# Where second-layer groups stand in the order of TensorE's work, in an attention and two-layer kernel

## The chip, the cores and the metric

The kernel runs on one core of one Trainium2 chip. The metric is the device time of one execution in microseconds (us). Before the change the median of three runs is 332.02 us (331.84 to 338.3). The engines are named as in the profile: PE is TensorE's matmuls and PEld its weight loads, ACT is ScalarE, DVE is VectorE, POOL is GpSimd, and SP is SyncE, which here only issues DMAs.

## The reference

Eight sequences (B) of 576 rows and eight heads (H) of width 64 go through causal attention with 16 extra ("beacon") keys in front. The result, 4608 tokens of width 512, goes through two matrix products with a leaky ReLU between them.

```python
k_all = np.concatenate([beacon_k, k], axis=2)
v_all = np.concatenate([beacon_v, v], axis=2)
scores = scale * np.matmul(q, k_all.transpose(0, 1, 3, 2))
scores = np.where(causal, -1000000000.0, scores)
scores = scores - scores.max(-1, keepdims=True)
a = np.exp(scores)
a /= a.sum(-1, keepdims=True) + 1e-09
attn_out = np.matmul(a, v_all)
x = attn_out.transpose(0, 2, 1, 3).reshape(B * S, H * D)
h = x @ w_in                       # 512 -> 2048
g = np.maximum(0.01 * h, h)
out = g @ w_out                    # 2048 -> 512
```

## The kernel before, in words

**Pairs.** Attention is worked in 32 pairs of heads, four to a sequence, numbered g = 0 to 31. Pairs 0 to 7 are written out as a string of steps (L756 to L764). From pair 8 on (`FIRST`), the score columns of all pairs, 1664 to a pair, are laid end to end and cut into tiles of 512. Three tiles make one `block` (L780), so there are 26 blocks, here B0 to B25. A block's score matmuls (L314) fill one tile in two single banks of PSUM (`apart`) and two tiles in two-bank buffers. ACT then takes the exponentials: of the first tile head by head (L329), of the other two at once for both heads (L333). POOL zeroes what lies above the diagonal (L289).

**Values.** `value(g, half)` multiplies probabilities with values (L359): 12 matmuls in the first half of a pair, 18 in the second. Each half takes one PSUM bank, which DVE empties (reciprocal L388, product L389). `x_turn(g)` then has SP write the transposed result into `xT` by two DMAs (L417, L425; three in the last sequence). Here V11.0 and V11.1 are the halves of pair 11.

**The two layers.** The 4608 tokens are nine chunks of 512. `up()` issues one first-layer group (`moe1`): four 512-column matmuls (L442, eight 256-column ones where a chunk wraps round in `xT`) into one PSUM bank, which ACT empties with the leaky ReLU into `gT` (L450). A chunk has 16 of them, here u2.0 to u2.15 for chunk 2. `down()` issues one second-layer group (`moe2`). Chunk 0 has 16 plain ones (L512). The others have 14, d2.0 to d2.13, from a Strassen-like scheme of seven products in two parts of eight 256-column matmuls each (L539). Products are added up in four banks: "a" is opened by group 0 and closed after group 5, "b" is open over groups 2 and 3, "c" from 6 to 11, "d" from 8 to 13. The left sides of some products are sums over `gT` that DVE makes (`token_sums`, L616): four additions for every eight first-layer groups, of which each later group issues one.

**PSUM.** Of the eight banks the two score buffers hold four. The other four (`ps_one`) are shared by first-layer groups, second-layer products, value halves and the two `apart` tiles of a block.

**Order.** The order on all engines is the order in which the program calls these functions (`manual_schedule`, L731), and each engine executes its own list in order. From pair 8 on a list of events with due times is sorted (L814) and walked: blocks, value halves, `x_turn`, the loads of queries, keys and values (`N`, `load_v_cast` on POOL's queue), the DMA transposes of queries and keys (`T`, on SP's queue) and `finish(g)`. Ahead of each event, `fill()` is called until the count of groups has reached a share of those that the sequence has to give (L820 to L823). `finish` of a sequence's last pair releases further chunks (`ready`): chunk 2 with pair 11, 3 with 15, 4 with 19, 5 with 23, 6 with 27, 7 and 8 with 31. `KEPT` groups are left over at a sequence's end.

`fill()` picks which kind of group is next. Before the change it alternates: a second-layer group is chosen after a first-layer one where both are possible (`turn`), and after a sequence's end up to `KEPT` second-layer groups come first (`held`). A first-layer group of chunk i needs chunk i-2 to be done in the second layer.

The lines that the prediction's steps touch: `fill` L598 to L610, `up` L625, `down` L636, `finish` L678 to L684, the loop L817 to L831, and the bank requests in `moe1` (L434), `moe2` (L535), `value` (L384) and `stretch` (L301).

Of the kernel before, what the change touches and what calls it, by code (L numbers as in the profile page):

```python
# [15 lines left out]
def kernel(  # L16
# [21 lines left out]
    NF = DF // 128  # L38
# [124 lines left out]
    def load_first_keys():  # L163
        for h in range(2):
            nc.sync.dma_start(out=first_k[h], in_=k[0, h].rearrange("(p i) d -> p i d", i=RI))
# [18 lines left out]
    def load_beacon_k(b0, b1, eng):  # L184
        eng.dma_start(out=bk_raw[:, b0:b1], in_=beacon_k[b0:b1].rearrange("b h n d -> (h n) b d"))
# [245 lines left out]
    def moe1(i, fc):  # L431
        if i not in gT:
            gT[i] = gpool.tile([128, NF, 512], BF16, name="gT")
        acc = ps_one.tile([128, 512], FP32, name="acc", tag="one")  # L434
        at = i * 512 % (XR * S)
        cut = min(512, XR * S - at)
        for lo, hi in ((0, cut), (cut, 512)):
            for j in range(NJ):
                if lo == hi:
                    continue  # L440
                x0 = (at + lo) % (XR * S)
                nc.tensor.matmul(  # L442
                    out=acc[:, lo:hi],
                    lhsT=w_in_cols(fc, j),
                    rhs=xT[:, j, x0 : x0 + hi - lo],
                    start=(j == 0),
                    stop=(j == NJ - 1),
                    skip_group_check=True,
                )
        nc.scalar.activation(out=gT[i][:, fc, :], in_=acc, func=AF.Prelu, alpha=0.01)  # L450
# [53 lines left out]
    def ND(i):  # L504
        return NF if i == 0 else 2 * len(PRODUCTS)
# [87 lines left out]
            in_=c.rearrange("p (t d) -> p t d", t=n),  # L593
        )

    done1, done2, at2, ready, turn, first_down, held = [0], [0], [0, 0], [0], [0], [0], [0]

    def fill():  # L598
        i1, fc = divmod(done1[0], NF)
        i2, n2 = at2  # L600
        can1 = i1 < ready[0] and (i1 < 2 or i2 > i1 - 2)
        can2 = i2 < NCH and i2 < i1 and done1[0] >= first_down[0]
        if held[0] and can2:
            held[0] -= 1
            down()
        elif can1 and (turn[0] == 0 or not can2):
            up()
        elif can2:
            down()
        return can1 or can2  # L610
# [3 lines left out]
    def add_due(n=1):  # L614
        while due and n:
            nc.vector.tensor_tensor(**due.pop(0)[1])  # L616
            n -= 1

    def add_all(i):
        while due and due[0][0] == i:  # L620
            add_due()
# [3 lines left out]
    def up():  # L625
        i1, n = divmod(done1[0], NF)
        assert i1 < ready[0]
        fc = n if i1 == 0 else n // 2 + n % 2 * HF
        moe1(i1, fc)
        add_due()  # L630
        done1[0] += 1
        turn[0] = 1
        if i1 and n % (2 * SLICE) == 2 * SLICE - 1:
            due.extend((i1, op) for op in token_sums(i1, n // 2 + 1 - SLICE, n // 2 + 1))

    def down():  # L636
        add_due()
        if at2[1] == 2:
            add_all(at2[0])
        moe2(*at2)  # L640
        done2[0] += 1
        at2[1] += 1
        if at2[1] == ND(at2[0]):
            at2[:] = at2[0] + 1, 0
        turn[0] = 0

    def unused(n, cols=128):
        ps = ps_one.tile([128, 512], FP32, name="av", tag="one")
# [16 lines left out]
            )  # L665

    NG = B * NPAIR
    KEPT = 3

    def has(g):  # L670
        return 0 <= g < NG
# [3 lines left out]
    def chunks_with(g):  # L675
        return (g + 1) // NPAIR * S // 512

    def finish(g, eng=0):  # L678
        if eng < 2 and g in xs:
            x_transposes(g, (dve, act)[eng])  # L680
        ready[0] = chunks_with(g)
        if g % NPAIR == NPAIR - 1:
            turn[0] = 1
            held[0] = KEPT  # L684

    def run(steps):
        for step in steps.split():
# [52 lines left out]
    with order:  # L740
        load_first_keys()
        load_beacon_k(0, 2, nc.scalar)
        nc.vector.memset(blank, 0.0)
        nc.vector.memset(ident, 0.0)
        run("l0.0 l1.0")
        make_identity(nc, ident, nomemset=True)
        make_ones()
        run("l1.1 l2.0 l2.1 V0.0 V0.1 l3.0 l3.1 V0.2 V0.3 V0.4 l4.0 l4.1 i0")
        make_pads()
        unused(13, 256)  # L750
        cast_beacon_k(0, 2, nc.scalar.copy)
        beacon_transposes(0, 2)
        unused(13)
        nc.scalar.copy(out=k_nat0[:, :, 0], in_=first_k[0])
        nc.vector.tensor_copy(out=k_nat0[:, :, 1], in_=first_k[1])
        run("q0.1 k0 w2.384 s0.0 m0.0 w3.256 s0.1 q1 s0.2 m0.1 k1 s0.3 m0.2")  # L756
        run("w2.384 s1.0 m1.0 q2 s1.1 k2 w2.384 s1.2 m1.1 w2.384 s1.3 m1.2 W0.0.4 s2.0 m2.0 W0.0.4 s2.1 W0.0.6 q3 l5.0 l5.1 s2.2 k3 w4.384 v0.0 m2.1 s2.3 i1 m2.2 W0.1.4 s3.0 m3.0 v1.0 s3.1 v0.1 s3.2 v1.1 m3.1 l6.0 l6.1 s3.3 x0.1 m3.2")
        run("v2.0 V1.0 V1.1 q4 v2.1 x1 k4.1 v3.0 v3.1 x2.1 s4.0 s4.1 x3 m4.0 V1.2 V1.3 V1.4 l7.0 l7.1 u u s4.2 s4.3 q5 k5 m4.1 m4.2 u o0 u")
        load_beacon_k(2, B, nc.gpsimd)
        run("s5.0 s5.1 m5.0 u u u s5.2 s5.3 q6 k6 m5.1 m5.2 o1 u u s6.0 s6.1 m6.0 u v4.0 u v4.1 y4 N8.0 N8.1 u s6.2 s6.3 q7 k7 m6.1 m6.2 u")  # L760
        cast_beacon_k(2, B, nc.gpsimd.tensor_copy)
        run("u v5.0 u v5.1 N9.0 s7.0 s7.1 m7.0 d x5 v6.0 v6.1 T8 d s7.2 s7.3")
        beacon_transposes(2, B)
        run("m7.1 m7.2 N9.1 u b8.2 b9.2 b10.2 b11.2 x6 v7.0 T9 v7.1 d d t0 d N10.0 N10.1 d V2.0 V2.1 x7 T10")  # L764


        FIRST = 2 * NPAIR
        COLS = FLAT[NKB]
        TILES = (NG - FIRST) * COLS // 512

        def tile_parts(n):
            at, end, parts = 512 * n, 512 * (n + 1), []
            while at < end:
                r, lo = divmod(at, COLS)
                hi = min(COLS, lo + end - at)
                parts.append((FIRST + r, lo, hi))
                at += hi - lo
            return parts

        def block(m):  # L780
            tiles = [tile_parts(n) for n in range(3 * m, min(3 * m + 3, TILES))]
            for n, parts in enumerate(tiles):
                stretch(parts, apart=n == 0)
            for parts in tiles:
                triangles(parts)

        def has_down():
            return at2[0] < done1[0] // NF

        since = 0  # L790
        events = []
        for g in range(FIRST, NG):
            if g > FIRST + 2:
                events.append((g - 2.75, 0, run, ("N%d.0" % g,)))
                events.append((g - 2.45, 0, run, ("N%d.1" % g,)))
            if g > FIRST + 2:
                events.append((g - 1.75, 0, run, ("T%d" % g,)))
            if g > FIRST + 3:
                events.append((g - 1.65, 0, run, ("b%d.2" % g,)))
            at = g + (2.05 if g % NPAIR == NPAIR - 1 else 2.25)  # L800
            events.append((at, 3, value, (g, 0)))
            events.append((at + 0.37, 4, value, (g, 1)))
            events.append((at + 0.38, 5, x_turn, (g,)))
        for m in range((TILES + 2) // 3):
            events.append((FIRST + (0.4 if m else 0.6) + 1536 / COLS * m, 2, block, (m,)))
        ends = [FIRST]
        for g in range(FIRST, NG):
            events.append((g + 3.5, 2, finish, (g, 2)))
            if g % NPAIR == NPAIR - 1:
                ends.append(g + 3.5)  # L810
        for b in range(2, B):
            for n in range(2 if b == 2 else 0, NKB):
                events.append((4 * b + (-0.4 if b == 2 else -0.9) + 0.3 * n, 6, load_v_cast, (b, n)))
        events.sort(key=lambda e: e[:2])  # L814
        first_down[0] = 4
        w, d0 = 0, done1[0] + done2[0]
        for at, _, what, args in events:  # L817
            while w + 2 < len(ends) and at > ends[w + 1]:
                w, d0 = w + 1, done1[0] + done2[0]
            todo = NF * ready[0] + sum(ND(i) for i in range(ready[0])) - KEPT - d0  # L820
            aim = d0 + todo * (at - ends[w]) / (ends[w + 1] - ends[w])
            while done1[0] + done2[0] < aim and fill():
                pass  # L823
            if what is block:
                since = done1[0] + done2[0]
            elif what is value and not has_down():
                while done1[0] + done2[0] < since + 4 and fill():
                    pass
            what(*args)
        while at2[0] < NCH:  # L830
            fill()  # L831
# [30 lines left out]
```

## Time and profile before

| what | value |
|---|---|
| median of three runs | 332.02 us |
| the profiled execution's own time | 332.48 us |
| its span, from the first to the last instruction | 330.8 us |
| granted TensorE clock | 0.999 |
| PE busy | 317.8 us |
| ACT busy | 199.8 us |
| POOL busy, DMA issues included | 183.2 us |
| DVE busy | 132.5 us |
| DMA packets | 155929, of them 143041 under 512 B |

A line of the timeline gives the start and the length in us, the engine, the line of the program, the operation, what it writes and reads, and how many instructions were merged. In square brackets stands the idle time of the engine before it, and what ended that. Ends of matmuls are modelled, so that a wait of PE is best read from the start of one matmul to the start of the next. A few matmul records are missing from the trace.

### The profile page before, as it was taken

Reading aid. Unit: us, or ns where it says so; the run is one execution under the profiler, and the core shown is the slowest. Engines: PE = TensorE matmul, PEld = TensorE weight load, DVE = VectorE, ACT = ScalarE, POOL = GpSimd, SP = SyncE. Lnnn points to the kernel's source line nnn. Section 1 sums busy time; section 2 is a strip of 40 time slices with the busy share of each in tenths; the row PEclk is TensorE's granted clock in tenths of the full one; section 3 lists DMA queues with packets and bytes.
Section 4 is the critical chain, followed back from the end, with each engine's and each line's share of the span. In section 5 each row is a group of like instructions: output and inputs, shape, how many; then the busy total and the mean of one; then the engine's idle time right before and its main releaser. Section 6 shows DMA issues by size and latency. Waiting matters only on the chain.

```text
span 330.8 us, 8482 instructions
## 1 busy us (share of the span) xinstructions
PE 317.8 (96%) x3401; PEld 213.1 (64%) x3429; DVE 132.5 (40%) x280; ACT 199.8 (60%) x336; POOL 183.2 (55%) x354
## 2 busy tenths in 40 slices
PE   8999999999899999999999999998999999999996
PEld 5574555455586557844778888655875695466685
DVE  3572357126443145414621453334442642333343
ACT  4969861678665784578645865587458514644420
POOL 8895968979987884669546976686221000000000
PEclk9999999999999999999999999999999999999999
DMA  8999999999999999999989999999431113000113
GB/s 134 140 204 178 153 209 121 179 181 131 180 111 169 158 157 142 131 164 102 145 122 154 109 146 113 184 120 155 55 100 37 36 21 127 2 0 34 64 43 117
DMA packets 155929, 39.93 MB, mean 121 GB/s; under 512 B 143041, under 2 KB 153153, under 8 KB 155889
## 3 DMA queue, kind: packets, MB, share of 16 engines
q0 software_dynamic: 99824, 18.54, 83.1%
q1 hardware_dynamic: 55792, 20.77, 38.7%
q8 instruction: 27, 0.44, 0.6%
q14 instruction: 14, 0.11, 0.1%
q10 hardware_dynamic: 272, 0.07, 0.1%
HBM read 37.22 MB, written 9.44 MB: 141 GB/s over the span
## 4 chain that ended last, share of the span: by engine, by line
PE 76%; DMA 8%; ACT 5%; DVE 4%; POOL 4%; issue 2%; SPq 0%; ACTq 0%; POOLq 0%
PE acc L442 34%; PE acc L539 25%; PE av L359 7%; PE sc L314 5%; DMA w_out_sb<-in_moe_w_out_dram 4%; PE acc L512 4%; DMA v_aug<-in_v_dram 3%; DVE gsum L616 2%; ACT aT L333 2%; ACT aT L329 2%; ACT gT L450 1%; DVE x_nat L389 1%; POOL gsum L158 1%; DMA xT<-x_nat 1%; POOL v_aug L214 1%
## 5 line engine op out<-in xcount | busy, mean ns | idle before, releaser
L442 PE MATMUL acc<-xT,w_in_sb 128*128 128x512 bf16 (+1 forms) x615 | 134.0, 357 | 1.9 <-DMA xT<-x_nat 0.5
L450 ACT ACTIVATE gT<-acc 128x512 bf16<-128x512 f32 x144 | 83.0, 620 | 56.9 <-PE acc L442 55.4
L442 PEld LDWEIGHTS <-w_in_sb 128*128 128x128 bf16 x640 | 59.6, 98 | 53.6 <-issue 4.3
L289 POOL TENSOR_SCALAR_AFFINE_SELECT aT<-aT 128x256 bf16<-128x256 bf16 (+2 forms) x160 | 59.8, 403 | 60.9 <-ACT aT L329 38.7
L539 PEld LDWEIGHTS <-gT 128*128 128x128 bf16 x512 | 48.9, 98 | 11.2 <-ACT gT L450 2.3
L333 ACT ACTIVATE aT<-sc 128x1024 bf16<-128x1024 f32 (+3 forms) x64 | 51.7, 890 | 0.0
L539 PE MATMUL acc<-w_out_sb,gT 128*128 128x256 bf16 x384 | 47.2, 273 | 1.4 <-ACT gT L450 1.3
L329 ACT ACTIVATE aT<-sc 128x512 bf16<-128x512 f32 (+3 forms) x64 | 28.9, 520 | 25.3 <-PE sc L314 25.3
L359 PEld LDWEIGHTS <-aT 128*128 128x128 bf16 (+1 forms) x960 | 36.6, 98 | 9.3 <-issue 3.0
L539 PEld LDWEIGHTS <-gsum 128*128 128x128 bf16 x384 | 36.1, 98 | 8.8 <-DVE gsum L616 3.3
L359 PE MATMUL av<-v_aug,aT 128*128 128x65 bf16 (+1 forms) x960 | 39.5, 194 | 1.9 <-ACT aT L329 1.6
L214 POOL DMA_DIRECT2D v_aug<-in_v_dram x40 | 34.3, 866 | 4.3 <-DMA w_in_sb<-in_moe_w_in_dram 4.0
L171 POOL DMA_DIRECT2D q_nat<-in_q_dram x48 | 34.9, 734 | 0.7
L171 POOL DMA_DIRECT2D k_nat<-in_k_dram x48 | 34.8, 732 | 0.7 <-DMA w_out_sb<-in_moe_w_out_dram 0.4
L539 PE MATMUL acc<-w_sum,gsum 128*128 128x256 bf16 x256 | 32.9, 273 | 1.8 <-DVE gsum L616 1.7
L616 DVE TENSOR_TENSOR gsum<-gT 128x1024 bf16<-128x1024 bf16 x16 | 11.2, 697 | 53.9 <-ACT gT L450 53.9
L389 DVE TENSOR_TENSOR x_nat<-av,rec 128x384 bf16<-128x384 f32 (+1 forms) x64 | 31.4, 490 | 2.2
L388 DVE RECIPROCAL rec<-av 128x6 f32<-128x6 f32 (+1 forms) x64 | 11.9, 185 | 50.7 <-PE av L359 50.5
L276 ACT ACTIVATE aT<-sc 128x1024 bf16<-128x1024 f32 (+3 forms) x32 | 26.0, 874 | 3.7 <-PE sc L267 1.9
L314 PE MATMUL sc<-qT,kT 64*128 64x80 bf16 (+22 forms) x384 | 22.4, 250 | 1.2 <-PE acc L442 0.5
L314 PEld LDWEIGHTS <-kT 64*128 64x128 bf16 x384 | 13.3, 94 | 11.9 <-issue 8.9
L573 DVE TENSOR_TENSOR u<-acc,u 128x512 f32<-128x512 f32 x8 | 5.5, 691 | 27.2 <-PE acc L539 27.2
(63 smaller groups left out, 221.5 us busy)
## 6 DMA issues: line engine op xcount, KB each, us to landing
out_dram<-osb SPq DMA_DIRECT2D x27, 256.0 KB, 2.8
q_nat<-in_q_dram POOLq DMA_DIRECT2D x48, 72.0 KB, 4.8
k_nat<-in_k_dram POOLq DMA_DIRECT2D x48, 72.0 KB, 5.2
v_aug<-in_v_dram POOLq DMA_DIRECT2D x24, 128.0 KB, 6.4
w_in_sb<-in_moe_w_in_dram POOLq DMA_DIRECT2D x2, 1024.0 KB, 12.3
w_out_sb<-in_moe_w_out_dram POOLq DMA_DIRECT2D x2, 1024.0 KB, 11.6
out_dram<-u SPq DMA_DIRECT2D x7, 256.0 KB, 2.3
gsum<-in_q_dram POOLq DMA_DIRECT2D x8, 144.0 KB, 6.4
```

The source lines that it names most:

```text
L171: nc.gpsimd.dma_start(out=t[:, :, par], in_=(q, k)[which][b, 2 * hp + par].rearrange("(t p) d -> p t d", p=NR),)
L214: nc.gpsimd.dma_start(out=dst[lo : ROWS[c], c, :, 0:D], in_=v[b, :, OFF[c] : OFF[c] + n].rearrange("h p d -> p h d"),)
L276: nc.scalar.activation(out=aT[:, :, c0 : c0 + w], in_=sc[:, :, 0:w], func=AF.Exp, scale=0.125)
L289: nc.gpsimd.affine_select(out=view, in_=view, compare_op=ALU.is_ge, fill=0.0, base=128 - n if lo == 0 else 0, channel_multiplier=-1, patte ...
L314: nc.tensor.matmul(out=(sc[par] if apart else sc[:, par])[:, at : at + b - a], lhsT=kT[ps_, c * 128 : (c + 1) * 128], rhs=qT[ps_, q0 : q0 ...
L329: nc.scalar.activation(out=probs[g][:, par, lo:hi], in_=sc[par][:, at : at + hi - lo], func=AF.Exp, scale=0.125)
L333: nc.scalar.activation(out=probs[g][:, :, lo:hi], in_=sc[:, :, at : at + hi - lo], func=AF.Exp, scale=0.125)
L359: nc.tensor.matmul(out=avv[:, n, 0 : D + 1], lhsT=aT[0 : ROWS[c], par, a0 : a0 + 128], rhs=va[0 : ROWS[c], c, 2 * hp + par, :], start=(c = ...
L389: nc.vector.tensor_tensor(out=x_nat[:, t0:t1].rearrange("p t e d -> p (t e) d"), in0=avv[:, :, 0:D], in1=rec[:, n0:n1, None].to_broadcast( ...
L442: nc.tensor.matmul(out=acc[:, lo:hi], lhsT=w_in_cols(fc, j), rhs=xT[:, j, x0 : x0 + hi - lo], start=(j == 0), stop=(j == NJ - 1), skip_gro ...
L450: nc.scalar.activation(out=gT[i][:, fc, :], in_=acc, func=AF.Prelu, alpha=0.01)
L539: nc.tensor.matmul(out=acc[:, lo : lo + HD], lhsT=left(i, n, fc, tile), rhs=right(n, fc), start=(opens and lo == 0 and fc == 0), stop=(fc ...
```

## The change

`fill()` no longer alternates. A counter `first` is set to 2 (`BEHIND`) at each block and at a sequence's end. While it is above zero, second-layer groups are chosen; otherwise first-layer groups as long as there are any, and second-layer groups after those. An exception (`kept`): the last two groups (`LAST`) of a chunk's second layer are not taken in this way while the next chunk's first layer still has groups to give. `KEPT` goes from 3 to 8. Ahead of a value half, at least three groups are issued since the last block, in all cases; before, it was four, and only where no second-layer group was at hand.

```diff
-    done1, done2, at2, ready, turn, first_down, held = [0], [0], [0, 0], [0], [0], [0], [0]
+    done1, done2, at2, ready, first_down, first = [0], [0], [0, 0], [0], [0], [0]
+
+    LAST, BEHIND = 2, 2
 
     def fill():
         i1, fc = divmod(done1[0], NF)
         i2, n2 = at2
         can1 = i1 < ready[0] and (i1 < 2 or i2 > i1 - 2)
         can2 = i2 < NCH and i2 < i1 and done1[0] >= first_down[0]
-        if held[0] and can2:
-            held[0] -= 1
+        kept = can1 and i1 == i2 + 1 and ND(i2) - n2 <= LAST
+        if first[0] and can2 and not kept:
+            first[0] -= 1
             down()
-        elif can1 and (turn[0] == 0 or not can2):
+        elif can1:
             up()
         elif can2:
             down()
...
-    KEPT = 3
+    KEPT = 8
...
         if g % NPAIR == NPAIR - 1:
-            turn[0] = 1
-            held[0] = KEPT
+            first[0] = BEHIND
...
             if what is block:
                 since = done1[0] + done2[0]
-            elif what is value and not has_down():
-                while done1[0] + done2[0] < since + 4 and fill():
+                first[0] = BEHIND
+            elif what is value:
+                while done1[0] + done2[0] < since + 3 and fill():
                     pass
             what(*args)
```

The lines left out set and clear `turn`, and define `has_down`. No instruction is added or removed; the same groups, blocks and value halves are issued in another order.

More of the change, by code (lines that the diff above doesn't have):

```diff
@@ L644, in down @@
             at2[:] = at2[0] + 1, 0
-        turn[0] = 0
     def unused(n, cols=128):
@@ L682, in finish @@
         if g % NPAIR == NPAIR - 1:
-            turn[0] = 1
-            held[0] = KEPT
+            first[0] = BEHIND
     def run(steps):
@@ L785, in block @@
                 triangles(parts)
-        def has_down():
-            return at2[0] < done1[0] // NF
         since = 0
```

## The prediction

> **What bounds the kernel.** I read the shares first, then PE's waits, then the timeline around blocks.
>
> ```profile
> PE 317.8 (96%) x3401; PEld 213.1 (64%) x3429; DVE 132.5 (40%) x280; ACT 199.8 (60%) x336; POOL 183.2 (55%) x354
> ...
> DMA  8999999999999999999989999999431113000113
> ```
>
> PE is the bound; no work is removed, so the change is worth only what it does to PE's 13 us of idle time. The DMA row matters too: nine tenths and more for 28 of 40 slices, to 231 us.
>
> PE's waits (who waited for whom: us in total, times, longest):
>
> ```profile
> PE acc L539 <- DVE gsum L616: 1.7, 5, 0.6
> PE av L359 <- ACT aT L329: 1.6, 3, 0.8
> PE acc L539 <- ACT gT L450: 1.3, 2, 0.7
> ...
> PE acc L442 <- DMA xT<-x_nat: 0.5, 1, 0.5
> PE sc L314 <- DMA kT<-k_nat: 0.4, 1, 0.4
> PE sc L314 <- DVE x_nat L389: 0.3, 1, 0.3
> PE acc L442 <- ACT aT L329: 0.2, 1, 0.2
> ```
>
> Each is small, and each row understates: an L539 matmul's row has 273 ns, while 16 in a run take 1.75 us, 109 each. So PE loses 0.16 more per wait than its idle time says.
>
> The second row has the pattern that the change is about, here at B15 (PE alone):
>
> ```profile
> 169.45 0.83 PE L314 MATMUL sc<-qT,kT 64*128 64x176 bf16 x14
> 171.08 0.53 PE L359 MATMUL av<-v_aug,aT 128*128 128x65 bf16 x12 [0.80 <-ACT aT L329]
> 171.45 0.82 PE L539 MATMUL acc<-w_sum,gT 128*128 128x256 bf16 x6
> ```
>
> Block, then a value half: d3.9 has just been issued, so products "c" and "d" hold two of the four shared banks, the block's first tile the other two, and V20.0 waits until an exponential has freed one. At B14 and B5 it is the same with "a" and "b" open. At B21, with nothing open, four first-layer groups follow and nothing waits (PE, then ACT):
>
> ```profile
> 218.09 3.63 PE L442 MATMUL acc<-xT,w_in_sb 128*128 128x512 bf16 x16
> 221.56 0.53 PE L359 MATMUL av<-v_aug,aT 128*128 128x65 bf16 x12
> 221.93 1.67 PE L442 MATMUL acc<-xT,w_in_sb 128*128 128x512 bf16 x7
> 223.65 0.72 PE L359 MATMUL av<-v_aug,aT 128*128 128x65 bf16 x18
> 224.21 0.60 PE L442 MATMUL acc<-xT,w_in_sb 128*128 128x512 bf16 x2
> ```
> ```profile
> 218.89 1.96 ACT L333 ACTIVATE aT<-sc 128x1024 bf16<-128x1024 f32 x2
> 220.70 2.11 ACT L450 ACTIVATE gT<-acc 128x512 bf16<-128x512 f32 x4
> ...
> 225.27 0.60 ACT L450 ACTIVATE gT<-acc 128x512 bf16<-128x512 f32 x1 [0.82 <-PE acc L442]
> ```
>
> These rows give my prices. A first-layer group takes (221.56 - 218.09)/4 = 0.87 of PE, a second-layer one 1.75/2, also 0.87. A value half takes 0.37 (221.56 to 221.93) or 0.56 (223.65 to 224.21), a block 0.77 (217.33 to 218.09). The group begun at 224.21 ends its slots at 225.08 and its bank is read out at 225.87; 0.05 for PE to restart makes **0.85 from a group's end to its bank's reuse**. Behind a block, ACT does exponentials first: the first group's bank is free at 221.30, **3.2 after the block's end**.
>
> **What goes.** From `fill` and the event loop I wrote down the order before and after. One stretch of each:
>
> ```
> before [B20] u5.0 u5.1 u5.2 u5.3 V25.0 u5.4 u5.5 V25.1 u5.6 [B21] u5.7 u5.8 u5.9 u5.10 V26.0 ...
> after  [B20] d4.8 d4.9 u5.1 V25.0 u5.2 u5.3 u5.4 V25.1 u5.5 [B21] d4.10 d4.11 u5.6 u5.7 V26.0 ...
> ```
>
> The five waits for sums go: two kept groups now stand between the last first-layer group of a chunk and the next chunk's d.0, which issue the additions in time. For the same reason the two waits of a d.0 for its activation go. The four waits for exponentials go, since three groups stand between a block and a value half; also the score matmul that waited for DVE at B5. B9's wait for keys goes because B9 comes later (below). That is thirteen: 1.7 + 1.6 + 1.3 + 0.4 + 0.3 + 0.2 = 5.5, with 13 x 0.16 = 2.1: **-7.6**.
>
> **What comes: open products.** Two second-layer groups at a time means that a chunk's fourteen are spread over several blocks, and their products stay open meanwhile. "c" and "d" are both open from d.8 to d.11. Before, no first-layer group ever stood there, except in the last chunks' alternation, where every second group needs no bank. After, u2.0 to u2.5 with B7 and B8 stand there, u3.0 to u3.9 with B12 and B13, u4.0 to u4.2 with B16, u5.1 to u5.5 with B21, u6.0 to u6.15 with B25. Two banks are left for groups, value halves and the block's first tile. What waits on PE there holds up all of PE, and so all that waits for it on ACT and DVE.
> - A block straight behind a first-layer group (B7, B8, B12, B13, B16, B21, B25) needs both banks, so it waits out that group's 0.85: 7 x 0.85 = 6.0.
> - A group behind a value half needs the bank of the group before the half: 0.85 less 0.37 is 0.48 (V13.0, 17.0, 18.0, 25.0, 29.0, 30.0, 31.0), or less 0.56 is 0.29 (V13.1, 16.1, 17.1, 25.1, 28.1, 29.1, 30.1): 7 x 0.48 + 7 x 0.29 = 5.4.
> - Two groups in a row lose nothing: 0.85 against 0.87.
>
> Together **+11.4**. The trace has no such place; the nearest are B14 and B15 (0.6 to 1.0 with two products open). The bounds are zero, if other waits already cover them, and 21 x 0.85 = 18. I take 11.4, as each term is a difference of rows.
>
> [...]
>
> **First-layer groups behind blocks.** Where only the two kept groups are left, the counter does nothing: B3, B4, B9, B17 and B22 are followed by three first-layer groups and a value half, with one product open, so three banks free. The half needs the first group's bank: 3.2 + 0.05 less 3 x 0.87 = 0.65. Before it was four groups and four banks, and zero. 5 x 0.65 = **+3.3** (zero to 4.3, if PE takes the whole 0.85).
>
> **The first sequence.** Eight kept instead of three means five groups fewer ahead of pair 11's end. B0 has one group fewer before it, but it waits in both cases for pair 8's keys, which land at 59.9: **+0.9**. From there, B2 is at 69.6 as before; B3 at 69.6 + 0.8 + 4 groups + two halves = 74.7; B4 with five groups and 0.65 at 81.4; B5 (four groups, 0.65) 87.3; B6 (five) 93.3; u2.0 (five) 99.3, its fourth matmul, which reads pair 11, at 100.0. Before that was 105.5, and it waited for this transfer (SP, then PE):
>
> ```profile
> 100.54 1.83 SPq L417 DMA_TRANSPOSE xT<-x_nat  x1
> 102.42 1.22 SPq L425 DMA_TRANSPOSE xT<-x_nat  x1
> ```
> ```profile
> 104.84 0.82 PE L442 MATMUL acc<-xT,w_in_sb 128*128 128x512 bf16 x3
> 106.19 1.02 PE L442 MATMUL acc<-xT,w_in_sb 128*128 128x512 bf16 x3 [0.53 <-DMA xT<-x_nat]
> ```
>
> V11.1's result was ready at 95.1; SP had pair 15's transposes ahead of it, which waited for keys that POOL issued at 91.69, 8.6 after B4's start, and that landed at 99.2. The chain hangs on B4 and on full DMA engines: 81.4 + 8.6 + (106.15 - 91.69) = 104.5. So u2.0 waits 4.5 in place of 0.7: **+3.8**. Bounds: with the latencies of the idle moment at 133 (1.1 from issue to landing for such a transpose, 3 for such a load) no wait, so -0.7; with a landing no earlier than before, +5.5.
>
> [...]
>
> **At nothing.** Loads and `T` keep their places among blocks; stores of a product go out later with it, which takes nothing from the queue that PE waits for. Five more groups stand behind the last pair: ACT's 0.60 lies under PE's 0.87 there, with three banks free; with one free bank it would be 0.85 for each of 16. The later deadlines for `xT` (u3.0 to u7.0) had 2.5 to 8 us in hand and lose 1 to 2; if one is missed, PE waits the rest.
>
> **Sum.** 11.4 + 3.3 + 0.9 + 3.8 - 7.6 = +11.8. Against the profiled execution's own 332.5 that is 344.3; it stood 0.5 above the median of 332.0, so **343.8**. The runs before spread from 331.8 to 338.3, so 2% (6.6 us) is about what can be told from no change.
>
> **Rivals.**
> 1. *Open products cost little: not slower.* For it: in the trace's alternating last chunks PE runs without waits while "c" and "d" are open. Against it: there every second group needs no bank. Place: the five stretches from d.8 to d.11; price: the 11.4, without which the sum is +0.4, 332.4. It decides within 2% when a place costs under 0.3 on average (21 x 0.3 = 6.2).
> 2. *Faster.* Neither pinch shows, and transfers come with the earlier blocks: -7.6 to -4.3, so 324.4 to 327.7. For it: thirteen waits do go. Against it: the DMA row.
> 3. *DMA holds the first sequence back further*: blocks B4 to B9 wait for keys too, which landed 0.5 to 3.6 before use. Each of six waiting 1 more gives 350.
> 4. *It doesn't do what it says*: 18 of 26 blocks get two second-layer groups behind them, six none. This is in the forecast; without those first-layer groups behind B3, B4, B9, B17 and B22 it would be 340.5.
>
> **How the numbers follow.** Forecast with its bounds, 337 to 349: 0.65. About even (rival 1, half the pinch), 331 to 337: 0.17. Faster, 324 to 331: 0.13. Above 349: 0.05. The range 331 to 349 takes the first two, 0.82. Slower by over 2% (above 338.7) has most of the forecast, 0.57, and rival 3: 0.62. Faster by over 2% (below 325.4) is the far end of rival 2: 0.04. Within 2%: 0.34.
>
> **What would show it.** Right: no waits of L539 for sums; score matmuls of B8, B12, B13, B16, B21, B25 waiting 0.7 to 0.9 for an L450; value halves behind B9, B17, B22 waiting about 0.6; u2.0's fourth matmul waiting 3 to 5 for `xT`. Wrong: blocks in the open stretches that start without a gap, a `xT` that lands by 101, or new waits of blocks for `kT`.

## The result, and the profile after

The changed kernel is **slower: 1.035 times the time before, 95% interval 1.025 to 1.046**. Its profiled execution took 344.46 us against 332.48 before, 11.98 longer; the forecast was 344.3 on that scale. (Its median of four, 348.2, contains two disturbed runs near 352, which the ratio leaves out.)

First the busy shares and the DMA row of the page after; a digit of the DMA row is a fortieth of the span, 8.6 us.

```profile
PE 324.0 (95%) x3429; PEld 215.2 (63%) x3429; DVE 133.0 (39%) x280; ACT 202.4 (59%) x336; POOL 185.3 (54%) x354
...
DMA  8999999999999999999999999999201030020123
```

The work is the same: PE's higher busy time comes mostly from the matmul records, all 3429 of which are present here, while 28 are missing from the trace before. DMA is about as full as it was for about as long (eight tenths or more in 28 slices of 8.6 us, before in 28 of 8.3). What has changed is PE's waits: their kinds have been exchanged. PE's waits after (us in total, times, longest):

```profile
PE acc L442 <- ACT gT L450: 3.4, 9, 0.7
PE sc L314 <- ACT gT L450: 3.0, 7, 0.5
PE av L359 <- ACT gT L450: 2.9, 6, 0.6
PE sc L314 <- DMA kT<-k_nat: 1.8, 2, 1.3
PE av L652 <- DVE blank L743: 1.1, 1, 1.1
PE acc L442 <- DMA xT<-x_nat: 0.9, 1, 0.9
```

L539, which had 3.0 us of waits before, is not in the list at all. The three rows that have come end with an ACT L450, that is with a bank of PSUM that a first-layer group had filled and ACT had to read out: one row for first-layer groups, one for blocks, one for value halves. The rows of B13's stretch, with products "c" and "d" open (timeline after, PE, then ACT):

```profile
150.18 0.81 PE L442 MATMUL acc<-xT,w_in_sb 128*128 128x512 bf16 x3
150.82 0.72 PE L359 MATMUL av<-v_aug,aT 128*128 128x65 bf16 x18
151.86 2.85 PE L442 MATMUL acc<-xT,w_in_sb 128*128 128x512 bf16 x12 [0.32 <-ACT gT L450]
154.55 0.53 PE L359 MATMUL av<-v_aug,aT 128*128 128x65 bf16 x12
155.40 1.02 PE L442 MATMUL acc<-xT,w_in_sb 128*128 128x512 bf16 x4 [0.32 <-ACT gT L450]
156.35 0.39 PE L314 MATMUL sc<-qT,kT 64*128 64x512 bf16 x1
157.11 0.59 PE L314 MATMUL sc<-qT,kT 64*128 64x512 bf16 x7 [0.37 <-ACT gT L450]
```
```profile
150.69 0.62 ACT L576 COPY p<-acc 128x512 f32<-128x512 f32 x1
151.15 0.65 ACT L450 ACTIVATE gT<-acc 128x512 bf16<-128x512 f32 x1
...
154.75 0.60 ACT L450 ACTIVATE gT<-acc 128x512 bf16<-128x512 f32 x1 [0.27 <-PE acc L442]
156.46 0.60 ACT L450 ACTIVATE gT<-acc 128x512 bf16<-128x512 f32 x1 [1.11 <-PE acc L442]
```

Each L450 row ends 0.05 to 0.06 before PE goes on: 151.80 and 151.86, 155.35 and 155.40, 157.06 and 157.11. V17.1's slots end at 150.82 + 0.56 = 151.38, so the group behind it starts 0.48 late, although the wait's own figure is 0.32. V18.0 costs its follower 155.40 - 154.92 = 0.48 as well. At B13 one score matmul is issued, and the next one, which needs the other bank, comes 0.76 later.

Going through the trace in this way, by starts and slots, PE's waits sum up to about 10.4 us before and about 21 after.

### The profile page after: what moved, and what is told of

Same layout as the page of the kernel before. It is cut to its first block, busy times and chain, and to the rows that moved or that the text cites. A ratio compares the mean times of both kernels' runs of the same rounds, so it can differ in the third digit from the quotient of the medians.

```text
span 342.7 us, 8502 instructions
## 1 busy us (share of the span) xinstructions
PE 324.0 (95%) x3429; PEld 215.2 (63%) x3429; DVE 133.0 (39%) x280; ACT 202.4 (59%) x336; POOL 185.3 (54%) x354
## 4 chain that ended last, share of the span: by engine, by line
PE 66%; DMA 12%; ACT 11%; POOL 6%; issue 2%; SPq 1%; DVE 0%; ACTq 0%; POOLq 0%
PE acc L442 28%; PE acc L539 24%; PE sc L314 5%; PE av L359 4%; ACT aT L333 4%; ACT gT L450 4%; DMA v_aug<-in_v_dram 4%; DMA w_in_sb<-in_moe_w_in_dram 4%; PE acc L512 3%; POOL aT L289 2%; DMA k_nat<-in_k_dram 2%; ACT aT L329 2%; DMA kT<-k_nat 1%; POOL v_aug L214 1%; POOL gsum L158 1%
## 5 line engine op out<-in xcount | busy, mean ns | idle before, releaser
L442 PE MATMUL acc<-xT,w_in_sb 128*128 128x512 bf16 (+1 forms) x640 | 135.3, 358 | 5.6 <-ACT gT L450 3.4
L450 ACT ACTIVATE gT<-acc 128x512 bf16<-128x512 f32 x144 | 85.1, 608 | 69.3 <-PE acc L442 68.9
L442 PEld LDWEIGHTS <-w_in_sb 128*128 128x128 bf16 x640 | 60.5, 98 | 58.9 <-issue 7.9
L289 POOL TENSOR_SCALAR_AFFINE_SELECT aT<-aT 128x256 bf16<-128x256 bf16 (+2 forms) x160 | 61.4, 414 | 65.6 <-ACT aT L329 40.9
L539 PEld LDWEIGHTS <-gT 128*128 128x128 bf16 x512 | 48.9, 98 | 7.9 <-issue 1.3
L539 PE MATMUL acc<-w_out_sb,gT 128*128 128x256 bf16 x384 | 46.1, 273 | 0.0
L539 PEld LDWEIGHTS <-gsum 128*128 128x128 bf16 x384 | 36.5, 98 | 5.5 <-issue 0.8
L539 PE MATMUL acc<-w_sum,gsum 128*128 128x256 bf16 x256 | 31.4, 273 | 0.0
L314 PE MATMUL sc<-qT,kT 64*128 64x80 bf16 (+21 forms) x384 | 24.4, 250 | 5.1 <-ACT gT L450 3.0
L314 PEld LDWEIGHTS <-kT 64*128 64x128 bf16 x384 | 14.0, 94 | 19.7 <-issue 14.6
L577 DVE TENSOR_TENSOR u<-u,p 128x512 f32<-128x512 f32 (+1 forms) x9 | 6.0, 671 | 27.0 <-ACT p L576 27.0
```

The costliest lines, as they stand in the source:

```text
L289: nc.gpsimd.affine_select(out=view, in_=view, compare_op=ALU.is_ge, fill=0.0, base=128 - n if lo == 0 else 0, channel_multiplier=-1, patte ...
L314: nc.tensor.matmul(out=(sc[par] if apart else sc[:, par])[:, at : at + b - a], lhsT=kT[ps_, c * 128 : (c + 1) * 128], rhs=qT[ps_, q0 : q0 ...
L442: nc.tensor.matmul(out=acc[:, lo:hi], lhsT=w_in_cols(fc, j), rhs=xT[:, j, x0 : x0 + hi - lo], start=(j == 0), stop=(j == NJ - 1), skip_gro ...
L539: nc.tensor.matmul(out=acc[:, lo : lo + HD], lhsT=left(i, n, fc, tile), rhs=right(n, fc), start=(opens and lo == 0 and fc == 0), stop=(fc ...
```

## The experiments

The theory after the result: the open products cost about 11 us, the three-group rule about 4, and the first sequence about 3. The rival explanations were that blocks and value halves wait for another reason which merely ends with an L450 (ACT being behind, the place of the block itself), and that most of the loss stems from keeping eight groups. All ratios below are to the kernel before.

**1. Own banks for all products.** The order is that of the changed kernel; every product but product 2 (which still adds to product 1's bank, open over groups 0 to 5) gets a bank that DVE or ACT empties as soon as its two groups are done, and partial sums are added from SBUF, one more DVE addition per chunk.

```diff
-        opens = n in (1, 6, 7, 5)
+        opens = n != 2
...
-            tt(out=part("u3"), in0=part("u3"), in1=c, op=ADD)
-            store(i, 1, 1, tiles, part("u3"))
+            o = kept("osb", 3)
+            tt(out=o, in0=part("u3"), in1=c, op=ADD)
+            store(i, 1, 1, tiles, o)
+            tt(out=c, in0=part("u2"), in1=c, op=ADD)
...
-            tt(out=c, in0=acc, in1=part("u2"), op=ADD)
+            tt(out=c, in0=acc, in1=part("u3"), op=ADD)
...
-            tt(out=c, in0=acc, in1=part("u2"), op=ADD)
+            tt(out=c, in0=acc, in1=part("p5"), op=ADD)
```

> The changed kernel with the same order of groups, but products 7, 4, 5 and 3 of the second layer each open and close a bank of their own; what was added up in PSUM is added by DVE instead (one more addition of about 0.7 us per chunk, off PE's path). No first-layer group then meets two open products. Theory (open products take the banks): the seven waits of blocks (4.7 us) and the fourteen of groups behind value halves (6.4 us) go, so about 11 us less than the changed kernel's 344.4: 333 to 335, at or a little above the kernel before. The waits behind B3, B4, B9, B17, B22 (about 0.7 each) stay. Rival A (ACT is simply late behind the blocks, whatever the banks): 343 to 345, unchanged. Rival B (the first sequence's transfers set the loss): unchanged up to u2.0 and at least 340.

Measured: 1.004 [0.999, 1.009], profiled 335.21. PE's waits in this kernel:

```profile
PE acc L442 <- DMA xT<-x_nat: 2.3, 1, 2.3
PE sc L314 <- DMA kT<-k_nat: 1.5, 1, 1.5
PE av L359 <- ACT gT L450: 1.3, 3, 0.6
```

No block waits for an L450 any more, and of the fourteen groups behind value halves one still waits (behind V13.0, 0.36) and two are 0.1 late. Three first-layer groups now wait 0.4 to 0.5 for DVE to empty a value half's bank. B3 and B4 still cost 0.77 and 0.69, as expected, but behind B9, B17 and B22, where product "d" was the open one, 0.3 to 0.4 is left. With the same order on PE, 9.3 us are gone with the open products (344.46 to 335.21). That is the cause of most of the loss. Some of what went came back elsewhere: `xT` lands 2.2 later than in the changed kernel (106.37 against 104.14), so that u2.0 waits 2.5 for it, and B0's wait for keys is followed by a stretch at half clock (0.50 from 61.00 to 64.40, last section).

**2. Close the products first.** Banks as in the changed kernel, but a chunk's second-layer groups 9 to 11 are issued ahead of any first-layer group, so that "c" and "d" are never both open while one is issued.

```diff
-        if first[0] and can2 and not kept:
+        if can2 and i2 and 9 <= n2 <= 11:
+            down()
+        elif first[0] and can2 and not kept:
```

> The changed kernel with one rule more: once group 8 of a chunk's second layer is issued, groups 9, 10 and 11 come next, so products c and d are never both open while a first-layer group is issued. Theory: the same 11 us go, but ten blocks in place of five are now followed by three first-layer groups and a value half at about 0.7 each: 344.4 - 11.1 + 3.5 = 337. Rival A: 343 to 345. Rival B: 340 or more.

Measured: 1.007 [1.004, 1.009], profiled 334.40, 2.6 below what was expected. The same cause taken away by other means, with the same outcome: no block waits for an L450. What is left is the other pinch, value halves behind three first-layer groups. PE's waits, and the stretch behind B3:

```profile
PE av L359 <- ACT gT L450: 5.5, 11, 0.6
```
```profile
75.42 2.77 PE L442 MATMUL acc<-xT,w_in_sb 128*128 128x512 bf16 x11
78.80 1.21 PE L359 MATMUL av<-v_aug,aT 128*128 128x65 bf16 x30 [0.61 <-ACT gT L450]
```

The three groups end at 75.42 + 3 x 0.87 = 78.03, the half starts at 78.80: 0.77. Ten such places cost 7.0. The expectation had not seen that u2.0 now stands behind B7, so that it finds `xT` landed: there is no row of waits for `xT`.

**3. Four groups behind a block**, as before the change.

```diff
-                while done1[0] + done2[0] < since + 3 and fill():
+                while done1[0] + done2[0] < since + 4 and fill():
```

> The changed kernel with four groups in place of three between a block and a value half. Theory (a fourth group gives ACT the time for the first one's bank): the five waits behind B3, B4, B9, B17, B22 go (3.6 us), the open products stay with seven block waits and twelve in place of fourteen waits behind value halves: 340. Rival (those value halves wait for the masks or the exponentials themselves): unchanged within 1, 343.5 to 344.5.

Measured: 1.027 [1.022, 1.032], profiled 342.08. The gain of 2.4 is about half of the expected 4.4 (to 340), and not for the expected reason alone. The value halves behind three groups do start on time (4.3 to 0.5 us). But with one product open and three banks free the fourth group needs the first one's bank as the half did, and the wait moves to it: 3.6 us in five waits of a first-layer group that follows another. PE's waits in this kernel:

```profile
PE acc L442 <- ACT gT L450: 4.5, 11, 0.6
PE sc L314 <- ACT gT L450: 3.0, 7, 0.5
PE sc L314 <- DVE x_nat L389: 2.0, 4, 1.0
```

The rest of the 2.4 comes from elsewhere: groups behind halves wait 4.2 instead of 6.4, and the keys at B6 and `xT` at u2.0 are there in time, while waits for DVE grow. Seven blocks still take 1.50 in place of 0.77 (B20 is one of them now, and B8 is not). So the figure of three is not what costs; the number of free banks is.

**4. Three groups kept over a sequence's end**, as before the change.

```diff
-    KEPT = 8
+    KEPT = 3
```

> The changed kernel with 3 in place of 8 groups kept over a sequence's end. By the order written down, no first-layer group then stands between groups 8 and 11 of a chunk, nine blocks are followed by three first-layer groups and a value half, and the first sequence has its five groups back. Theory: -11.1 for the open products, +2.8 for four more such halves, -1.5 to -2.5 for the first sequence: 333.5 to 335. Rival B (the loss is the first sequence's transfers alone): 339 to 340, with block waits as before.

Measured: 1.027 [1.019, 1.034], profiled 341.19; expected was 333.5 to 335. This is the miss of the study. The half that was about banks came true: no block waits for an L450. PE's waits:

```profile
PE acc L442 <- DMA xT<-x_nat: 4.7, 1, 4.7
PE av L359 <- ACT gT L450: 4.1, 8, 0.6
PE acc L442 <- ACT gT L450: 1.5, 2, 0.7
```

But the five groups that are no longer kept went ahead of pair 11's end. B4 starts 2.2 later than in the changed kernel (85.03 against 82.83) and `xT` lands 4.8 later (108.93 against 104.14), while PE comes to u2.0's fourth matmul only 1.0 later (104.1 against 103.1): there it waits 4.9. And PE did not go on at full speed. In the table by windows, the second number is PE's busy time, and the granted clock (`PEclk`) is the third number from the end:

```profile
104.00:108.80 4.80, 0.27 (x2) 0.00 (x0) 0.50 (x2) 0.00 (x0) 1.07 (x2) 0.78 1.44 155
108.80:113.00 4.20, 3.81 (x21) 1.56 (x23) 0.00 (x0) 2.27 (x5) 0.00 (x0) 0.50 0.72 168
113.00:117.00 4.00, 4.00 (x29) 2.02 (x28) 0.76 (x2) 3.43 (x7) 3.63 (x8) 0.94 0.50 82
```

If the clock was either full or half, these three means put the half from about 106.7 to 113.5. PE worked for about 4.5 of these 6.8 us, so about 2.2 was lost (an estimate, half of the 4.5). With the wait's 4.9 that is 7.1, as much as the expectation lacks (6.2 to 7.7).

**5. Own banks and closing together**, with two more groups of chunk 0 left over, which was to leave no block followed by three first-layer groups with a product open (`ND(i2) - n2 <= (LAST if i2 else 4)`; otherwise the edits of 1 and 2).

> The changed kernel with the banks of their own, the rule that groups 9 to 11 follow group 8, and the last four groups (one whole tile) of chunk 0 kept in place of its last two. By the order written down, no block in the loop is then followed by three first-layer groups with a product open. Theory: what the change was to gain stays (the waits for sums, activations and exponentials, 7.6 us) and its price goes: the closing rule alone measured 334.3, of which ten waits of 0.7 go, so 327 to 328.5, 1 to 1.5% under the kernel before. Rival A (PE is held by something else as soon as these waits go, such as keys or masks): 331 to 334.

Measured: **0.995 [0.993, 0.998]**, profiled 331.25: a little faster than both kernels, but 3 to 4 us short of the expectation. PE's waits:

```profile
PE sc L314 <- DMA kT<-k_nat: 2.0, 3, 1.1
...
PE sc L314 <- DVE x_nat L389: 1.0, 2, 0.8
PE av L359 <- ACT gT L450: 0.9, 4, 0.3
```

The waits for banks are all but gone. In their place blocks wait for keys (2.5 us by starts) and for DVE (1.7), because PE now reaches them earlier: total waits are 8.4 against 10.4 before the change. What two groups behind each block could win in waits is thus about 2 us.

**6. As 5, with no group kept for the next chunk's beginning** (`LAST, BEHIND = 0, 2`).

> The kernel of e5_both, but with none of a chunk's last groups kept (LAST = 0, chunk 0 unchanged). Theory (the two kept groups are what took the waits for sums and activations away): at chunks 2 to 6 the second layer's first groups follow the first layer's last ones again; five waits of L539 for sums of about 0.55 and three for an activation of 0.3 to 0.9 come back: 4 to 5 us above e5_both, 331.5 to 333. Rival (those waits were only shifted by the other order): within 1 us of e5_both.

Measured: 0.995 [0.991, 0.998], profiled 331.58, level with 5. PE's waits of L539 in this kernel, all that came back:

```profile
PE acc L539 <- ACT gT L450: 0.7, 1, 0.7
...
PE acc L539 <- DVE gsum L623: 0.2, 1, 0.2
```

That is d3.0 and d3.2, 0.9 and 0.4 by starts. (Chunk 0 still leaves its four over.) Elsewhere blocks and value halves between the groups give ACT and DVE the time. So the waits for sums went mainly because of the new order as such and not because of the exception for the last two groups, to which the prediction had put them down.

**7. As 5, with three groups kept instead of eight.**

> The kernel of e5_both with 3 in place of 8 groups kept over a sequence's end. The open products play no part in either, so this is the first sequence alone. Theory (pair 11's transposed result lands 21 to 24 us after block B4 begins, whatever PE does): u2.0 stands ahead of B7 and comes 19 us after B4, so it waits 2 to 5 us for xT, which e5_both, with u2.0 behind B7, doesn't: 2 to 5 us above e5_both, and more if PE's clock drops in that wait as in e4_kept_three. Rival (my prediction's own step: five groups more ahead of pair 11's end give back 4.7 us): 323 to 325.

Measured: 1.008 [1.004, 1.012], profiled 334.18, 3 to 4 above 5. PE's timeline and the table by windows:

```profile
101.77 0.81 PE L442 MATMUL acc<-xT,w_in_sb 128*128 128x512 bf16 x3
106.82 2.32 PE L442 MATMUL acc<-xT,w_in_sb 128*128 128x512 bf16 x5 [4.24 <-DMA xT<-x_nat]
```
```profile
103.30:106.70 3.40, 0.00 (x0) 0.00 (x0) 0.47 (x2) 0.00 (x0) 0.31 (x1) 1.00 1.89 199
106.70:110.10 3.40, 3.28 (x19) 1.43 (x21) 0.00 (x0) 1.52 (x3) 0.00 (x0) 0.50 0.92 223
110.10:113.50 3.40, 3.40 (x30) 1.66 (x26) 0.02 (x1) 3.40 (x7) 2.28 (x6) 1.00 0.37 70
```

u2.0 waits 4.4 and is followed by one stretch of 3.4 us at half clock (0.50), with PE busy for 3.3 of it, which is an estimated 1.6 us of work lost. With the products closed, keeping eight is a gain of 3 to 4 us.

**8. Own banks in the kernel before**, as a control for experiment 1.

> The kernel before with banks of their own for products 7, 4, 5 and 3, in its own order. A control for e1_own_bank: only V20.0 behind B15, which met products c and d open, should lose its wait of 1.0; those behind B5 and B14 (a and b open) stay. So 331, the same as before within 0.5%. If the additions on DVE or the other banks had an effect of their own, it would show here as well: 328 or less, or 334 or more.

Measured: 0.999 [0.994, 1.003], profiled 333.34. By itself the edit gives nothing; the 9.3 us of experiment 1 are those of the new order with open products. The waits for sums and for activations stay, and so do those for exponentials behind B5 and B14; only V20.0 behind B15, which had met "c" and "d" open, starts 0.19 late in place of 1.06, as expected:

```profile
PE acc L539 <- ACT gT L450: 2.0, 3, 0.7
PE acc L539 <- DVE gsum L618: 1.7, 5, 0.6
...
PE av L359 <- ACT aT L329: 0.8, 2, 0.5
```

## Why the prediction was right

The forecast was right in sign and size, and its largest term for the reason given. That the sum agrees within 0.2 us is luck: single terms are off by up to 3.4 us, in both directions. The table sets its terms beside the trace after, read by starts and slots, in us.

| term of the sum | predicted | measured |
|---|---|---|
| seven blocks with "c" and "d" open | +6.0 | +5.1 |
| groups behind value halves with "c" and "d" open | +5.4 | +6.4 |
| value halves behind three first-layer groups | +3.3 | +4.3 |
| B0, one group less before it included | +0.9 | +1.8 |
| u2.0 and `xT` of pair 11 | +3.8 | +0.4 |
| B6, for DVE and keys | 0 | +1.2 |
| waits removed | -7.6 | -7.7 |
| rest | 0 | +0.5 |
| sum | +11.8 | +12.0 |

**Open products: right, and shown.** All seven blocks named wait: from the first score matmul to what follows the block they take 1.50, and the others mostly 0.77, so each loses 0.73. All fourteen groups wait too (0.48 or 0.49 behind most first halves, 0.29 behind most second ones; the five of 0.29 are too short for a row in the list of waits). Experiments 1 and 2 remove the cause in two ways, and the waits go with it. The terms were mis-sized in two details. The price of 0.85 from a group's end to its bank's reuse holds at B13 too (155.40 + 0.87 = 156.27 to 157.11, so 0.84), but a block does not stand still meanwhile: its first score matmul needs only the bank that is free, so that the block ends 0.73 late. And behind V13.0, V17.1, V25.0 and V29.1 it is 0.66, 0.48, 0.86 and 0.48 in place of the 0.48, 0.29, 0.48 and 0.29 worked out. In these four places ACT copies product 5 (L576, 0.62 to 0.64) ahead of the group's L450, as in the ACT rows above at 150.69; behind V16.1 and V28.1, where no such copy stands, it is 0.29. Rival 1 is out; experiment 1 shows what its case would have looked like, 335 and not 332, as some of the gain is lost again at transfers.

**Value halves behind three groups: right.** B3, B4, B9, B17 and B22 give 0.77, 0.69, 0.73, 0.66 and 0.73 for the 0.65 told; some second halves add 0.7 together. But the step read the pinch as the price of three groups in place of four. Experiment 3 shows that a fourth group hides nothing when one product is open: it waits for the same bank.

**The first sequence: the landing right, the wait wrong.** `xT` landed at 104.14 (told: 104.5), but u2.0's fourth matmul was reached by PE at 103.1 and not at 100.0, and waited 1.1 and not 4.5. The timeline after, PE, then SP:

```profile
102.43 0.81 PE L442 MATMUL acc<-xT,w_in_sb 128*128 128x512 bf16 x3
104.18 0.38 PE L442 MATMUL acc<-xT,w_in_sb 128*128 128x512 bf16 x1 [0.94 <-DMA xT<-x_nat]
```
```profile
99.00 1.22 SPq L417 DMA_TRANSPOSE xT<-x_nat  x1
100.27 1.22 SPq L425 DMA_TRANSPOSE xT<-x_nat  x1
```

The step that failed is the schedule of blocks from B0 on, which let PE lose nothing ahead of u2.0 but 0.65 a block. B0 started 0.94 late, as its keys landed at 60.8 and not at 59.9 as before; B3 to B6 were 1.1, 1.4, 1.6 and 1.8 behind the times told; B6 then waited 0.5 for DVE and 0.7 for the keys of pair 14, which the prediction had only as rival 3, in a larger form, and as one of its signs of being wrong. So PE came 3.1 late to a transfer at which it would have had to wait, and the loss was paid earlier in small sums. The landing hung on B4 as told, though not at a constant distance: it came 21.3 after B4's start here, 23.1 before the change, and 22.0, 23.9 and 24.2 in experiments 1, 4 and 5. The 4.5 us wait exists: it shows in experiments 4 and 7, where fewer groups are kept. That overturns the reading of which part is to blame. The prediction put this wait down to keeping eight; by the runs it is longest where three are kept (4.9 and 4.4, against 1.1 here and 2.5 in experiment 1), and with eight kept and the products closed first (experiments 2, 5 and 6) u2.0 stands behind B7 and does not wait at all.

**Removed waits: right in sum.** All of L539's waits and the four for exponentials have gone, and B9's for keys. The cause given for the waits for sums, two groups left over, holds for one chunk only, in the order of experiments 5 and 6.

**Rivals 2 to 4.** Faster needed both pinches to be absent; with both largely taken away the kernel was 0.5% faster and not 1.4 to 2.4% (experiment 5), since transfers did not come earlier by as much as PE did (blocks waited 2.5 us for keys). The order came out as written down, so rival 4 is what the forecast held it to be: blocks with two second-layer groups behind them where there are any.

What stays open: 0.5 us of the sum, which lies behind B0, as B0's term holds all that is lost up to its start (0.94 later, with one group of 0.87 less done); and why the distance from B4 to the landing varies by 2.9 us, for which no run was made.

## What to carry to other kernels

An accumulation that stays open over several steps takes its bank away from all else that rotates through the pool: before work is spread out between other work, count the banks that remain free at each place, and price a place that runs short by the time from a group's end to its bank's reuse (here 0.85, less whatever PE does meanwhile). If the spreading is wanted, close the accumulations first, in banks of their own or without other groups in between; here that, with two more groups of chunk 0 left over, turned 3.5% slower into 0.5% faster. And when PE is brought forward to a transfer that is bound elsewhere, the gain ends there as a wait; where that wait was 4.70 and 4.24 us (experiments 4 and 7), part of the work behind it also ran at half clock (next section).

## What the runs showed of the hardware that was not expected

In three of the profiled executions, of experiments 1, 4 and 7, PE's granted clock went down to 0.50 around a wait, and the work behind the wait took longer. In experiment 7, with 4.24 us of waiting, it was 1.00 from 103.30 to 106.70, 0.50 from 106.70 to 110.10 and 1.00 from there to 113.50 (the table there). The five matmuls of L442 that begin at 106.82 end their slots at 109.07, where the next block starts: 0.45 each, while the 0.87 of a first-layer group with its four makes 0.22. In experiment 4, with 4.70 us of waiting, the clock was at half for about 6.8 us (worked out there from the means of its windows).

In experiment 1 PE was not idle all along: the two waits at B0 (0.60 and 1.63 by starts) left it busy for 1.49 of 3.40 us, and the stretch behind had half the clock, an estimated 1.7 us of work lost, as PE was busy in all of it (windows, then PE's timeline):

```profile
57.60:61.00 3.40, 1.49 (x8) 0.50 (x8) 2.02 (x3) 0.60 (x1) 3.40 (x5) 1.00 1.93 167
61.00:64.40 3.40, 3.40 (x17) 1.22 (x17) 0.00 (x0) 2.83 (x4) 3.32 (x6) 0.50 1.79 199
```
```profile
59.08 0.38 PE L442 MATMUL acc<-xT,w_in_sb 128*128 128x512 bf16 x1 [0.44 <-DVE xT L410]
60.92 1.45 PE L314 MATMUL sc<-qT,kT 64*128 64x512 bf16 x12 [1.47 <-DMA kT<-k_nat]
```

In the changed kernel itself much the same waits at the same place (0.60 and 1.42) brought no drop; the mean clock of its span is 1.000. The same two windows there:

```profile
57.60:61.00 3.40, 1.71 (x10) 0.55 (x9) 2.24 (x4) 0.60 (x1) 3.40 (x5) 1.00 1.92 166
61.00:64.40 3.40, 3.40 (x25) 1.60 (x26) 0.00 (x0) 2.92 (x4) 3.40 (x6) 1.00 1.86 200
```

So 1.49 us of work in 3.40 was followed by half clock in one run, and 1.71 by full clock in another. What decided it is not shown: no run varied the length or the position of a wait alone.
